# Casts of paired projections three slots apart, maxima's scores behind the first scores, values' bank copied by ScalarE, and single-bank PSUM tiles in the first and last phase of an attention and MLP kernel

## The chip, the cores and the metric

One core of a Trainium2 chip. The metric is the device time of one execution in microseconds (us); several executions are measured and the median is quoted. The core has five engines with a queue of instructions each: TensorE (PE in the profile; PEld is its loading of weights, which overlaps matmuls), VectorE (DVE), ScalarE (ACT), GpSimd (POOL) and SyncE (SP, which here only issues DMAs). Matmul results go to PSUM, which this kernel treats as eight banks of [128, 512] fp32; everything else lies in SBUF. A kernel written in the Tile language states which tile an instruction reads and writes, and the scheduler sets the semaphores: an instruction that writes a tile waits for the readers of what was there before.

## The reference, cut to what matters

S = 2048 tokens, D = 512, 32 heads of 16, window 256, MLP width 1792, all in fp32:

```python
xn = layernorm(x)
q, k, v = heads(xn @ wqkv)                       # H = 32, Dh = 16
scores = q @ k.T * 16 ** -0.5
scores = where(0 <= i - j < 256, scores, -1e9)   # i: query, j: key
s = heads_back(softmax(scores) @ v) @ wo
h = gelu(layernorm(xn) @ w1 + b1)                # tanh form of GELU
g = silu(h @ w2 + b2)
out = x + s * g
```

Both branches start from `xn`; the MLP branch normalises it once more.

## The kernel before, in words

**Precision.** Every product of activations and weights is made of three passes (`PASSES`, line 66): an operand is split by `split` (68) into a high part in `fp32r` and the low rest, and high x high, high x low and low x high are summed in PSUM. So each projection is 4 x 3 = 12 matmuls for a block of 128 x 512.

**Order.** All instructions are issued through `Ordered` (32 to 46), which holds TensorE, VectorE, ScalarE and GpSimd to the order of the program; only SP's queue is ordered by the scheduler. Since that helper records every operation, all rows of the profile carry its line, L42, and are told apart by the tiles' names. The order of the work is written out by hand in slots: a main loop over steps t = -16 to 128 (616 to 635), with two lists of work for each step. `fills[t, half]` holds matmuls that fill TensorE between the attention's own (projections, and later the first blocks of the MLP), `plan[t]` holds the rest (`at`, 523). A step of the loop issues, in this order: the scores and exponential of the second pair of heads (`prob_block(…, 1)`), the first half of the fill, the row maxima of the step 12 ahead (`max_block`, m = t + 12), the second half of the fill, the plan's entries, `prob_block(…, 0)`, and the values of the step before (`pv_step`).

**First phase (head, t < 0).** Layer norm of `x` by chunks of 512 tokens, transposes (`job_x`, 183), projections of the first group of four heads (`job_qk`, 239) and of the values (`job_v`, 277). There are eight groups of four heads (`NQ`); queries and keys of a group lie in a slot `qk0` or `qk1`, used in turn.

**Attention steps (t = 0 to 127).** 16 steps for each group, one for each block of 128 tokens. A step makes the scores of 128 keys against up to 384 queries transposed, into `stb` (`prob_block`, 425), the exponential by ScalarE into `pt`, and POOL masks `pt` by `affine_select`. The maximum of each row goes into the product as further rows of `qk`; `max_block` (384) makes it ahead: eight score matmuls, those of the farthest key block (`first`) into `zo`, the others into `xy`; then VectorE's `copy_predicated` merges the two under the triangular mask and `tensor_reduce` makes the maximum. After every fourth block `max_rows` (409) sends the rows to `qk` by way of DRAM. `pv_step` (446) multiplies the values with `pt` into `otb`, a part of `zo`'s second bank, VectorE copies `otb` to `oraw`, and every fourth step a DMA takes it to `oT_d`. The last 12 steps have no maxima left, and there every second scores go to `xy`.

**The paired projections.** From the second group on, two chunks are projected in tandem (`tandem`, 351): 64 contracted rows at a time, one chunk in the upper half of TensorE's rows and the other in the lower, into `fb[0]` and `fb[1]`. Each ends in `finish` (305): ScalarE copies the bank to `raw` (a tile of the pool `t2`, five buffers). Then `high` casts it to `fp32r` into `sh` and issues four DMAs of 128 KB into `qk` (from the third group on one of 16 KB more), and `low` lets POOL subtract into `sl` and issues two DMAs. `sh` and `sl` have one buffer each. When `high` and `low` run is set by lines 323 and 324, `at(t + 1 + c % 2, …)`: the plan of the first step after the pair's end for the even chunk, of the second for the odd one. There are 14 pairs of chunks (seven groups, two pairs each; spans in 576 to 579).

**PSUM before.** One pool holds eight banks for the whole run (153 to 157): `xy`, `zo` and `stb` are tiles of two banks, `fb[0]` and `fb[1]` of one. `bank()` (160) gives the two halves of `stb` in turn, or `fb[0]` and `fb[1]`. In the head `stb` serves transposes (kt 0 and 1) and values, then the attention's scores; the transposes of kt 2 and 3 go to `zo[:, 1]` and to `xy[:, 0]` or `fb`.

**Last phase (from 641).** The MLP by four chunks of 512 tokens, 14 blocks of hidden units each. `hidden` (688) makes a block in a half of `stb`, `activate` (693) applies GELU on ScalarE and splits on VectorE, `project` (702) adds its product with `w2` onto four accumulators, `accs = [xy[:, 0], xy[:, 1], zo[:, 0], fb[0]]` (684). At the end of a chunk (748 to 773) VectorE adds `b2` onto the accumulators, ScalarE applies SiLU (`gate`, two buffers in turn), TensorE transposes the next chunk's `y` into `zo[:, 1]` and `fb[1]` (`y_transpose`, 502), and four output products of 12 matmuls each go to halves of `stb`; each is multiplied by its gate on VectorE, added to `x` on POOL and sent out. Here "a boundary" is the stretch from the last `project` of a chunk to the first `project` of the next.

Of the kernel before, what the change touches and what calls it, by code (L numbers as in the profile page):

```python
# [9 lines left out]
F32 = mybir.dt.float32  # L10
# [8 lines left out]
P = 128  # L19
# [4 lines left out]
NQ = H // 4  # L24
# [25 lines left out]
def mixer_kernel(ctx, tc, x, wqk, wv, wo, w1, b1, w2, b2, out):  # L50
# [6 lines left out]
    t2 = ctx.enter_context(tc.tile_pool(name="t2", bufs=5))  # L57
    small = ctx.enter_context(tc.tile_pool(name="small", bufs=3))
    dram = ctx.enter_context(tc.tile_pool(name="dram", bufs=1, space=bass.MemoryType.DRAM))
    psum = ctx.enter_context(tc.tile_pool(name="psum", bufs=1, space=PSUM))  # L60
    attn = ExitStack()
    vp = attn.enter_context(tc.tile_pool(name="vp", bufs=1))
    pp = attn.enter_context(tc.tile_pool(name="pp", bufs=8))
    sgp = attn.enter_context(tc.tile_pool(name="sgp", bufs=1))
# [88 lines left out]
    xy = psum.tile([P, 2, 512], F32, name="xy")  # L153
    zo = psum.tile([P, 2, 512], F32, name="zo")
    otb = zo[:, 1, 256:384]
    stb = psum.tile([P, 2, 512], F32, name="stb")
    fb = [psum.tile([P, 512], F32, name=f"fb{i}") for i in range(2)]
    turn = {"st": 0, "fb": 0}

    def bank(kind="st"):  # L160

        turn[kind] ^= 1
        return stb[:, turn[kind]] if kind == "st" else fb[turn[kind]]

    vt = vp.tile([P, NKB, 16, DH + 1], F32, name="vt")

# [8 lines left out]
    mhalf = const.tile([P, 4], F32, name="mhalf")  # L175
    negc = const.tile([P, 1], F32, name="negc")
    nc.vector.memset(negc, NEG)
    mask = upper.bitcast(I32).unsqueeze(1).unsqueeze(1).to_broadcast([P, 2, 2, P])
    neg = negc.unsqueeze(2).unsqueeze(2).to_broadcast([P, 2, 2, P])
    b1s = const.tile([P, NF], F32, name="b1s")  # L180
# [2 lines left out]
    def job_x(c):  # L183
        box = []

        def mm(k):
            kt, i = k // 4, k % 4
            if i == 0:
                box.append(bank() if kt < 2 else zo[:, 1] if kt == 2 else xy[:, 0] if c == 0 else bank("fb"))
            nc.tensor.transpose(box[kt][:, P * i: P * (i + 1)], xs[c][i][:, P * kt: P * (kt + 1)], ident)  # L190
            if i == 3:
                sl = slice(512 * c, 512 * (c + 1))
                split(big[:, 0, kt, sl], big[:, 1, kt, sl], box[kt])
        return [(109, mm, k) for k in range(16)], lambda: None
# [44 lines left out]
    def job_qk(n, c):  # L239

        box = []
        ops = [(kt, a, b) for kt in range(KT) for a, b in PASSES]
        sl = slice(512 * c, 512 * (c + 1))

        def mm(i):
            if i == 0:
                box.append(bank("fb"))
            kt, a, b = ops[i]
            nc.tensor.matmul(box[0], wqs[n][:, a, kt], big[:, b, kt, sl],
                             start=(i == 0), stop=(i == len(ops) - 1))  # L250

        def send(src, qk, tt):
            copy_rows(slots[n % 2][tt:P:4, qk, :, sl], src[64 * qk: 64 * qk + 64])

        def finish():
            hi = sgp.tile([P, 512], F32R, tag="sh", name=f"sh_{n}_{c}")
            lo = sgp.tile([P, 512], F32R, tag="sl", name=f"sl_{n}_{c}")
            raw = t2.tile([P, 512], F32, tag="t2", name=f"pjr_{n}_{c}")
            nc.scalar.copy(raw, box[0])

            def high():
                nc.scalar.copy(hi, raw)
                if n >= 2:
                    copy_rows(slots[n % 2][3:P:32, 0, :, sl], slots[n % 2][7:P:32, 0, :, sl])
                for qk, tt in ((1, 0), (0, 0), (1, 2), (0, 1)):
                    send(hi, qk, tt)

            def low():
                (nc.gpsimd if n else nc.vector).tensor_tensor(lo, raw, hi.bitcast(F32), op=ALU.subtract)
                send(lo, 1, 1)  # L270
                send(lo, 0, 2)

            later(1 if n else 0, high)
            later(3 if n else 1, low)
        return [(216, mm, i) for i in range(len(ops))], finish

    def job_v(hf, i):

        box = []

        def mm(k):
            if k == 0:
                box.append(bank().rearrange("p (b d) -> p b d", b=2))
            j, kt, (a, b) = k // 12, k % 12 // 3, PASSES[k % 3]
            kb = 2 * i + j
            nc.tensor.matmul(box[0][:, j], big[:, a, kt, P * kb: P * (kb + 1)], wva[:, b, kt],
                             start=(k % 12 == 0), stop=(k % 12 == 11))

        def finish():
            nc.scalar.copy(vt[:, 2 * i: 2 * i + 2, :, 0:DH], box[0].rearrange("p b (h d) -> p b h d", d=DH))  # L290
        return [(109, mm, k) for k in range(24)], finish

    def pair_qk(n, c):

        ops = [(kt, a, b) for kt in range(KT) for a, b in PASSES]
        sl = slice(512 * c, 512 * (c + 1))

        def mm(ps, i, r, **flags):
            kt, a, b = ops[i]
            nc.tensor.matmul(ps, wqs[n][r, a, kt], big[r, b, kt, sl], **flags)  # L300

        def send(src, qk, tt):
            copy_rows(slots[n % 2][tt:P:4, qk, :, sl], src[64 * qk: 64 * qk + 64])

        def finish(ps, t):
            hi = sgp.tile([P, 512], F32R, tag="sh", name=f"sh_{n}_{c}")
            lo = sgp.tile([P, 512], F32R, tag="sl", name=f"sl_{n}_{c}")
            raw = t2.tile([P, 512], F32, tag="t2", name=f"pjr_{n}_{c}")
            nc.scalar.copy(raw, ps)

            def high():
                nc.scalar.copy(hi, raw)
                if n >= 2:
                    copy_rows(slots[n % 2][3:P:32, 0, :, sl], slots[n % 2][7:P:32, 0, :, sl])
                for qk, tt in ((1, 0), (0, 0), (1, 2), (0, 1)):
                    send(hi, qk, tt)

            def low():
                nc.gpsimd.tensor_tensor(lo, raw, hi.bitcast(F32), op=ALU.subtract)
                send(lo, 1, 1)  # L320
                send(lo, 0, 2)

            at(t + 1 + c % 2, high)
            at(t + 1 + c % 2, low)
        return 3 * KT, mm, finish

    def pair_v(i):
# [56 lines left out]
    def max_block(n, qb):  # L384
# [10 lines left out]
                         (xy[:, a, 256 * p + off: 256 * (p + 1)], slice(P * lo, P * (qb + 1))))  # L395
            nc.tensor.matmul(out, slot[r, 0, p, P * qb: P * (qb + 1)], slot[r, 1, p, keys], start=True, stop=True)

        for p, a, first in ((0, 1, True), (0, 0, False), (1, 1, True), (1, 0, False),
                            (0, 1, False), (1, 1, False), (0, 0, True), (1, 0, True)):
            if qb >= 2 or not first:  # L400
                scores(p, a, first)
        four = xy.rearrange("q a (p k) -> q a p k", p=2)
# [22 lines left out]
    def prob_block(n, kb, p):  # L425
        slot = slots[n % 2]
        w = min(384, S - P * kb)
        pt = pp.tile([P, 2, 384], F32, tag="pt", name=f"pt_{n}_{kb}_{p}")
        both = xy if p and 16 * n + kb + LEAD >= 16 * NQ else stb
        for a in (1, 0):  # L430
            r = slice(64 * a, 64 * a + 64)
            nc.tensor.matmul(both[:, a, 0:w], slot[r, 1, p, P * kb: P * (kb + 1)],
# [13 lines left out]
    def pv_step(n, qb):  # L446
# [7 lines left out]
                                 skip_group_check=True, tile_position=(0, 32 * j))  # L454
        if qb % 4 == 0:
            outs[0] = sgp.tile([P, 512], F32, tag="or", name=f"oraw_{n}_{qb}", bufs=2)
        nc.vector.tensor_copy(outs[0][:, P * (qb % 4): P * (qb % 4 + 1)], otb)
        if qb % 4 == 3:
            nc.sync.dma_start(oT_d[n // 2, n % 2::2, :, P * (qb - 3): P * (qb + 1)], outs[0])

# [41 lines left out]
    def y_transpose(c, kt, ps=None):  # L502
        ts = mlp["y"]
        if ps is None:
            ps = zo[:, 1] if kt % 2 else fb[1]
        for i in range(4):
            nc.tensor.transpose(ps[:, P * i: P * (i + 1)], ts[i][:, P * kt: P * (kt + 1)], ident)
        split(mlp["yy"][0][kt], mlp["yy"][1][kt], ps)
# [108 lines left out]
    for t in range(-16, end + 1):  # L617
        m = t + LEAD
        if t == -5:
            open_slot(1)  # L620
            clear_rows(1)
        if 0 <= t < end:
            prob_block(t // 16, t % 16, 1)
        fill_in(t, 0)
        if 0 <= m < end:
            max_block(m // 16, m % 16)
        fill_in(t, 1)
        for fn, args in plan.get(t, []):
            fn(*args)
# [11 lines left out]
    open_w2(1)  # L641
    gated = bigp.tile([P, 2, 512], F32, tag="wa", name="gated")
    attn.close()
    cp = ctx.enter_context(tc.tile_pool(name="cp", bufs=1))
    gp = ctx.enter_context(tc.tile_pool(name="gp", bufs=2))
    mlp["yp"] = ctx.enter_context(tc.tile_pool(name="yp", bufs=4))
    b2s = cp.tile([P, 512], F32, name="b2s")
    nc.sync.dma_start(b1s, b1)
    early = {}
    for f in range(0, EARLY, 2):  # L650
        t = gp.tile([P, 2, 512], F32, tag="ohl", name=f"hr_{f}", bufs=4)
        nc.sync.dma_start(t, h_d[f: f + 2].rearrange("f p t -> p f t"))
        early.update({f + 2: t[:, 0], f + 3: t[:, 1]})
    nc.sync.dma_start(b2s, bass.AP(tensor=b2.tensor, offset=b2.offset, ap=[[0, P], [1, 512]]))
    wos = cp.tile([P, 2, 4, 512], F32R, name="wos")
    for f in range(W2_FIRST, W2_FIRST + 2):
# [24 lines left out]
        return ohl  # L681

    for c in range(NCH):
        accs = [xy[:, 0], xy[:, 1], zo[:, 0], fb[0]]
        gs, os_, hs = {}, [], {}
        made = early if c == 0 else {}

        def hidden(f):
            hs[f] = bank()
            for k in range(3 * KT):  # L690
                hidden_mm(hs[f], f, k)

# [9 lines left out]
        def project(f):  # L702
            gh, gl = gs.pop(f)
            for i in range(4):
                acc = accs[i]
                sl = slice(P * i, P * (i + 1))
                for k, (a, b) in enumerate(((gh, 0), (gh, 1), (gl, 0))):
                    nc.tensor.matmul(acc, a[:, sl], w2_part(b, f), start=(f == 0 and k == 0),
# [4 lines left out]
        for f in range(NF + 1):  # L713
# [31 lines left out]
                os_.append(split_o(c, f - 11, *wanted))  # L745
            if 10 <= f < 14:
                wanted = load_o(c, f - 10)
        us = [accs[i] for i in range(4)]
        for u in us:
            nc.vector.tensor_add(u, u, b2s)  # L750

# [5 lines left out]
        for i in range(4):  # L757
# [2 lines left out]
                    y_transpose(c + 1, 2 * i + kt)  # L760
            tok = 512 * c + P * i
            xt = load(t2, "t2", x[tok: tok + P, :], f"xo_{c}_{i}")
            ps = bank()
            k = 0
            for g in range(4):
                for a, b in PASSES:
# [40 lines left out]
```

## Time and profile before

| | |
|---|---|
| three runs | 961.39, 955.6, 956.57 us; median 956.57 us |
| the profiled execution's own time | 956.07 us |
| its span on the core, mean granted TensorE clock | 954.3 us, 0.939 of full speed |
| busy over the span: PE, PEld | 800.4 us (84%), 615.7 us |
| DVE, ACT, POOL | 491.7 us (52%), 349.8 us (37%), 289.1 us (30%) |
| DMA | 29% of 16 engines' span, 84 GB/s |

By stage (times from the span's start): the head is 0 to 85.81 us, the attention steps 85.81 to 538.40, the first MLP chunk with the loading of the last weights 538.40 to 651.70, and the rest, three chunks and the four ends, 651.70 to 954.30.

How rows are read. A row of the busy time by stage has the stretch, its length, then busy us and instructions of PE, PEld, DVE, ACT and POOL, then the mean granted clock, the share of DMA and GB/s. A row of the waits has the waiting group, what it waited for, the us lost in sum, how often, and the mean of one. A row in order of time has the start, the duration, the engine, the instruction with its tiles (out<-in) and shape, how many are grouped, and in brackets how long the engine stood idle before it and for whom. A row of the groups has the busy time and the mean of one in ns, then the idle time before them and for whom.

### The profile page before, as it was taken

How to read it: one execution, taken by the hardware profiler on the slowest of the kernel's cores; microseconds unless marked ns; L12 is line 12 of the kernel's file. 1: busy time of each engine (PE TensorE's matmuls, PEld its weight loads, DVE VectorE, ACT ScalarE, POOL GpSimd, SP SyncE). 2: the span in 40 equal slices, each digit the busy share in tenths (PEclk: the TensorE clock that was granted, in tenths of full speed). 3: DMA queues.
4: the chain of work that ended last, by engine and by line, in shares of the span. 5: the costliest groups of instructions: out<-in, count | busy, mean ns of one | idle time of the engine just before them, and what ended most of it. 6: DMA issues, size and time to landing. Idle time of an engine off the chain costs nothing. (4 is left out here: it accounts for less than half of the span.)

```text
span 954.3 us, 18265 instructions
## 1 busy us (share of the span) xinstructions
PE 800.4 (84%) x7384; PEld 615.7 (65%) x7384; DVE 491.7 (52%) x866; ACT 349.8 (37%) x515; POOL 289.1 (30%) x575
## 2 busy tenths in 40 slices
PE   4789887778889888887788889579996899779995
PEld 4677555555667667555565578457885688658883
DVE  6666656667656556666676275421543144521242
ACT  5523545545555454544557622211111111111110
POOL 4001544545454344554565400120012101120012
PEclk9889989989999999888799999889999999899999
DMA  8332343332452223335415352420013001210022
GB/s 289 86 64 64 82 103 105 91 86 67 105 126 50 72 54 112 92 82 133 116 37 156 115 176 89 132 78 12 23 46 125 28 5 40 89 44 1 23 76 79
DMA packets 51476, 79.97 MB, mean 84 GB/s; under 512 B 10112, under 2 KB 14208, under 8 KB 51392
## 3 DMA queue, kind: packets, MB, share of 16 engines
q1 hardware_dynamic: 51392, 78.80, 29.0%
q8 instruction: 58, 0.95, 0.5%
q14 instruction: 26, 0.21, 0.1%
HBM read 35.13 MB, written 15.99 MB: 54 GB/s over the span
## 5 line engine op out<-in xcount | busy, mean ns | idle before, releaser
L42 POOL TENSOR_SCALAR_AFFINE_SELECT pt<-pt 128x256 f32<-128x256 f32 x480 | 188.5, 418 | 223.1 <-ACT pt L42 222.2
L42 ACT ACTIVATE pt<-stb 128x768 f32<-128x768 f32 (+1 forms) x244 | 189.0, 775 | 163.4 <-PE stb L42 153.8
L42 DVE TENSOR_REDUCE mt<-xy 128x4 f32<-128x1024 f32 (+1 forms) x128 | 152.6, 1192 | 4.4
L42 DVE COPY_PREDICATED xy<-upper,zo 128x512 f32<-128x512 int32 x112 | 78.0, 696 | 141.5 <-PE zo L42 136.8
L42 PE MATMUL stb<-yh,w1s 128*128 128x512 f32 x400 | 132.6, 394 | 7.6 <-ACT g L42 5.0
L42 PE MATMUL stb<-qk 64*128 64x384 f32 (+1 forms) x488 | 101.7, 409 | 42.0 <-ACT pt L42 38.9
L42 PE MATMUL zo<-pt,vt 128*17 128x128 f32 x2880 | 109.2, 285 | 23.8 <-DVE xy L42 21.2
L42 PE MATMUL fb<-xnT,wqb 64*128 64x512 f32 (+1 forms) x720 | 129.1, 425 | 0.0
L42 DVE CAST gh<-g 128x512 fp32r<-128x512 f32 x56 | 26.9, 480 | 165.1 <-ACT g L42 155.6
L42 PEld LDWEIGHTS zo<-pt,vt 128*17 128x17 f32 x2880 | 70.0, 100 | 64.1 <-DVE xy L42 51.6
L42 ACT ACTIVATE g<-stb,b1s 128x512 f32<-128x512 f32 x50 | 34.0, 689 | 205.1 <-PE stb L42 201.8
L42 PEld LDWEIGHTS stb<-qk 64*128 64x128 f32 x488 | 49.3, 196 | 80.0 <-ACT pt L42 69.5
L42 PE MATMUL xy<-qk 64*128 64x256 f32 (+2 forms) x536 | 90.6, 320 | 3.9 <-DMA qk<-sl 3.5
L42 PEld LDWEIGHTS stb<-yh,w1s 128*128 128x128 f32 x400 | 75.9, 190 | 26.2 <-ACT g L42 6.3
L42 PEld LDWEIGHTS zo<-qk 64*128 64x128 f32 x448 | 70.5, 203 | 25.6 <-DVE oraw L42 19.0
L42 PEld LDWEIGHTS xy<-qk 64*128 64x128 f32 x536 | 75.3, 204 | 8.7 <-issue 5.3
L42 PE MATMUL zo<-qk 64*128 64x128 f32 x448 | 74.7, 270 | 6.1 <-DVE oraw L42 5.6
L42 PE MATMUL stb<-w1s 128*128 128x512 f32 x200 | 78.6, 393 | 0.0
L42 PE MATMUL xy<-w,gh 128*128 128x512 f32 x224 | 70.3, 394 | 9.1 <-DVE gh L42 4.4
L42 PEld LDWEIGHTS fb<-xnT,wqb 64*128 64x128 f32 (+1 forms) x720 | 73.2, 202 | 4.9
L42 POOL TENSOR_TENSOR or<-or,rec 128x512 f32<-128x512 f32 x16 | 20.5, 1284 | 150.2 <-DMA rec<-rden_d 134.4
L42 PE MATMUL stb<-wos,ohl 128*128 128x512 f32 x192 | 56.7, 450 | 9.8 <-DVE gated L42 9.0
(108 smaller groups left out, 1045.2 us busy)
## 6 DMA issues: line engine op xcount, KB each, us to landing
qk<-sh SPq DMA_DIRECT2D x128, 128.0 KB
qk<-sl SPq DMA_DIRECT2D x64, 128.0 KB
oT_d<-oraw SPq DMA_DIRECT2D x32, 256.0 KB
x<-in_x_dram SPq DMA_DIRECT2D x16, 256.0 KB
or<-oT_d SPq DMA_DIRECT2D x16, 256.0 KB
rec<-rden_d SPq DMA_DIRECT2D x16, 256.0 KB
xo<-in_x_dram SPq DMA_DIRECT2D x16, 256.0 KB
out_dram<-xo SPq DMA_DIRECT2D x16, 256.0 KB
```

Of the source, the lines that this page charges most:

```text
L42: r = issue(*args, **kwargs)
```

## The change

Four things, in the one file:

- **Casts.** `high` and `low` of the odd chunk of a pair run in the plan of the fourth step after the pair's end instead of the second.
- **Maxima.** `max_block` is called right behind `prob_block(…, 1)`, ahead of the fill's first half. Its eight matmuls are reordered: the four into `xy` first, the four into `zo` last.
- **Copy.** `oraw<-otb` is made by ScalarE; `otb` is cleared once at the start.
- **PSUM.** The pool of the attention now ends with it. In the head two tiles of one bank (`ps_st`) serve the transposes kt 0 and 1 and the values; the transposes kt 2 and 3 go to `fb` in turn with the projections. At t = 0 these two tiles give way to the two-bank `stb`. In the last phase three pools of two tiles each take the eight banks: `ps_mx` (two banks a tile, the four accumulators), `ps_st` (one bank: hidden blocks and output products) and `ps_yt` (one bank: the transposes of `y`). The dictionary `early` is renamed `ready`.

```diff
-    psum = ctx.enter_context(tc.tile_pool(name="psum", bufs=1, space=PSUM))
     attn = ExitStack()
+    psum = attn.enter_context(tc.tile_pool(name="psum", bufs=1, space=PSUM))
...
-    stb = psum.tile([P, 2, 512], F32, name="stb")
     fb = [psum.tile([P, 512], F32, name=f"fb{i}") for i in range(2)]
-    turn = {"st": 0, "fb": 0}
-
-    def bank(kind="st"):
-
-        turn[kind] ^= 1
-        return stb[:, turn[kind]] if kind == "st" else fb[turn[kind]]
+    early = ExitStack()
+    ps_st = early.enter_context(tc.tile_pool(name="ps_st", bufs=2, space=PSUM))
+    stb = []
+    turn = [0]
+
+    def fill_bank():
+
+        turn[0] ^= 1
+        return fb[turn[0]]
...
+    nc.vector.memset(otb, 0.0)
...
-                box.append(bank() if kt < 2 else zo[:, 1] if kt == 2 else xy[:, 0] if c == 0 else bank("fb"))
+                box.append(ps_st.tile([P, 512], F32, tag="b", name=f"tr_{c}_{kt}") if kt < 2 else fill_bank())
...
-                box.append(bank("fb"))
+                box.append(fill_bank())
...
-                box.append(bank().rearrange("p (b d) -> p b d", b=2))
+                box.append(ps_st.tile([P, 2, 256], F32, tag="b", name=f"pv_{hf}_{i}"))
...
-            at(t + 1 + c % 2, high)
-            at(t + 1 + c % 2, low)
+            at(t + 1 + 3 * (c % 2), high)
+            at(t + 1 + 3 * (c % 2), low)
...
-        for p, a, first in ((0, 1, True), (0, 0, False), (1, 1, True), (1, 0, False),
-                            (0, 1, False), (1, 1, False), (0, 0, True), (1, 0, True)):
+        for p, a, first in ((0, 1, False), (0, 0, False), (1, 1, False), (1, 0, False),
+                            (0, 1, True), (0, 0, True), (1, 1, True), (1, 0, True)):
...
-        both = xy if p and 16 * n + kb + LEAD >= 16 * NQ else stb
+        both = xy if p and 16 * n + kb + LEAD >= 16 * NQ else stb[0]
...
-        nc.vector.tensor_copy(outs[0][:, P * (qb % 4): P * (qb % 4 + 1)], otb)
+        nc.scalar.copy(outs[0][:, P * (qb % 4): P * (qb % 4 + 1)], otb)
...
-            ps = zo[:, 1] if kt % 2 else fb[1]
+            ps = ps_yt.tile([P, 512], F32, tag="b", name=f"yt_{c}_{kt}")
...
         if 0 <= t < end:
+            if t == 0:
+                early.close()
+                stb.append(attn.enter_context(tc.tile_pool(name="ps_s2", bufs=1, space=PSUM)).tile(
+                    [P, 2, 512], F32, name="stb"))
             prob_block(t // 16, t % 16, 1)
-        fill_in(t, 0)
         if 0 <= m < end:
             max_block(m // 16, m % 16)
+        fill_in(t, 0)
         fill_in(t, 1)
...
     attn.close()
+    ps_mx = ctx.enter_context(tc.tile_pool(name="ps_mx", bufs=2, space=PSUM))
+    ps_st = ctx.enter_context(tc.tile_pool(name="ps_st", bufs=2, space=PSUM))
+    ps_yt = ctx.enter_context(tc.tile_pool(name="ps_yt", bufs=2, space=PSUM))
...
-        accs = [xy[:, 0], xy[:, 1], zo[:, 0], fb[0]]
+        accs = [ps_mx.tile([P, 2, 512], F32, tag="mx", name=f"acc_{c}_{i}") for i in range(2)]
...
-            hs[f] = bank()
+            hs[f] = ps_st.tile([P, 512], F32, tag="b", name=f"h_{c}_{f}")
...
-                acc = accs[i]
+                acc = accs[i // 2][:, i % 2]
...
-            ps = bank()
+            ps = ps_st.tile([P, 512], F32, tag="b", name=f"s_{c}_{i}")
```

More of the change, by code (lines that the diff above doesn't have):

```diff
@@ L648, in mixer_kernel @@
     nc.sync.dma_start(b1s, b1)
-    early = {}
+    ready = {}
     for f in range(0, EARLY, 2):
@@ L652, in mixer_kernel @@
         nc.sync.dma_start(t, h_d[f: f + 2].rearrange("f p t -> p f t"))
-        early.update({f + 2: t[:, 0], f + 3: t[:, 1]})
+        ready.update({f + 2: t[:, 0], f + 3: t[:, 1]})
     nc.sync.dma_start(b2s, bass.AP(tensor=b2.tensor, offset=b2.offset, ap=[[0, P], [1, 512]]))
@@ L683, in mixer_kernel @@
     for c in range(NCH):
-        accs = [xy[:, 0], xy[:, 1], zo[:, 0], fb[0]]
+        accs = [ps_mx.tile([P, 2, 512], F32, tag="mx", name=f"acc_{c}_{i}") for i in range(2)]
         gs, os_, hs = {}, [], {}
-        made = early if c == 0 else {}
+        made = ready if c == 0 else {}
         def hidden(f):
-            hs[f] = bank()
+            hs[f] = ps_st.tile([P, 512], F32, tag="b", name=f"h_{c}_{f}")
             for k in range(3 * KT):
@@ L747, in mixer_kernel @@
                 wanted = load_o(c, f - 10)
-        us = [accs[i] for i in range(4)]
+        us = [accs[i // 2][:, i % 2] for i in range(4)]
         for u in us:
```

## Prediction

> **What bounds the kernel now.** I read the page first, then the busy time by stage (windows), then who waited for whom in each stage, and last the order in time around the longest waits.
>
> ```profile
> core 0: us, PE busy (x) PEld busy (x) DVE busy (x) ACT busy (x) POOL busy (x), PEclk, DMA share, GB/s
> 0.00:85.81 85.81, 64.36 (x412) 53.95 (x414) 52.20 (x100) 33.37 (x53) 10.91 (x22) 0.92 0.48 136
> 85.81:538.40 452.59, 377.00 (x5438) 274.00 (x5434) 282.61 (x484) 244.20 (x354) 230.59 (x514) 0.92 0.35 92
> 651.70:719.78 68.08, 68.08 (x302) 56.30 (x301) 28.65 (x58) 10.14 (x14) 5.88 (x5) 1.00 0.11 34
> 719.78:756.80 37.02, 25.31 (x107) 19.38 (x106) 10.66 (x17) 7.07 (x11) 6.40 (x5) 0.95 0.23 80
> 823.50:861.94 38.44, 25.89 (x101) 19.63 (x100) 10.28 (x16) 6.38 (x10) 6.40 (x5) 0.87 0.14 53
> ```
>
> TensorE is the busiest engine. The stages differ. Inside an MLP chunk (651.70 to 719.78) it is never idle and the clock granted is 1.00, so nothing is to be had there. Between two chunks (the last two rows) it is busy about 25 of 37 to 38 us. In the attention steps (85.81 to 538.40, 128 steps) and in the head it loses 75 and 21 us, at a mean clock of 0.92. The change touches these three.
>
> Who waits in the attention steps, and one such wait in order of time:
>
> ```profile
> ACT sh L42 <- DMA qk<-sh: 38.2, 14, 3.7
> PE stb L42 <- ACT pt L42: 38.9, 27, 3.4
> PE zo L42 <- DVE xy L42: 21.2, 58, 0.7
> ```
> ```profile
> 304.67 0.61 ACT L42 CAST sh<-pjr 128x512 fp32r<-128x512 f32 x1
> 311.16 0.62 ACT L42 CAST sh<-pjr 128x512 fp32r<-128x512 f32 x1 [3.00 <-DMA qk<-sh]
> 312.54 0.38 PE L42 MATMUL stb<-qk 64*128 64x256 f32 x2 [2.45 <-ACT pt L42]
> ```
>
> The reader should see a queue. The second cast of a pair comes one step after the first into the same buffer `sh`, whose four transfers are not done; ScalarE stands 3.00 us, the exponential behind the cast is late, and the next scores, which need the bank that it reads, leave TensorE idle for 2.45. There are 14 such casts, one per pair of projections. What one costs in whole steps (start of one exponential to that of another, two steps each):
>
> ```profile
> 116.20:122.24 6.04, 5.49 (x88) 3.89 (x84) 4.76 (x10) 4.62 (x8) 3.77 (x9) 1.00 0.11 14
> 122.24:133.82 11.58, 7.99 (x90) 5.74 (x88) 4.67 (x9) 3.77 (x6) 4.95 (x11) 0.73 0.61 157
> 445.52:452.54 7.02, 4.17 (x52) 2.28 (x48) 5.29 (x9) 4.62 (x7) 4.43 (x10) 0.94 0.52 149
> 452.54:462.56 10.02, 6.79 (x72) 4.64 (x72) 4.93 (x11) 3.76 (x5) 4.29 (x9) 0.50 0.62 161
> ```
>
> The first such place costs 11.58 - 6.04 = 5.5, the last 10.02 - 7.02 = 3.0; part is the wait, part the clock, which falls after it (0.73, 0.50). Over 13 of the 14 places, each against the two steps ahead of it, it comes to 46 us. The 14th, step 4, is held by something else (below).
>
> **The casts three slots apart.** The high cast and the subtraction of the odd job move from two steps after the pair's end to four; the even job's stay at one. With them go six transfers of 128 KB and, from the third group on, one of 16 KB. On SP's queue they go behind a transfer of row maxima and one of `oT_d`; on POOL the subtraction goes behind the masks of two more steps; the raw tile is held two steps longer in a pool of five, of which at most three are live then. From 304.67 to 311.16 the buffer was busy 6.5 us; three steps of 3.0 us (6.04 / 2) are 9, so the wait ends before the cast comes. Once (steps 50 and 52) only two steps lie between: up to 1 us left. If all goes, 46 us; if only TensorE's idle time goes, 38.2 x 2.45 / 3.00 = 31. I take 46, since half of a place's price is the clock that falls with it.
>
> What comes late instead is the data. A chunk's odd half is first read six to thirteen steps after the old cast, except in the first group (old cast in step 4, new in step 6, read in step 8). Step 4 shows how long that takes:
>
> ```profile
> 96.48 0.61 ACT L42 CAST sh<-pjr 128x512 fp32r<-128x512 f32 x1
> 102.84 0.44 PE L42 MATMUL xy<-qk 64*128 64x128 f32 x4 [3.49 <-DMA qk<-sl]
> ```
>
> 6.4 us from cast to use; from the plan's place in step 6 to the start of step 8 are some 5 us (one step and two thirds), so about 1.5 us at step 8. In step 4 the maxima's scores now stand ahead of the fill, which no longer covers: 0.5. Together 2 us lost (0 to 5).
>
> **Maxima behind the first scores; the bank copied by ScalarE.** The order of instructions on TensorE changes from scores, fill, maxima's scores, fill, scores, values to scores, maxima's scores, fill, fill, scores, values; the maxima's eight matmuls write `xy` first and `zo` last. VectorE's masked copy then has both fills as cover before the values need `zo`. In the row above TensorE lost 21.2 us to that copy, but most of that is not on the path: the next scores wait for the second exponential anyway.
>
> ```profile
> 302.35 0.83 ACT L42 ACTIVATE pt<-stb 128x768 f32<-128x768 f32 x1
> 302.62 0.85 PE L42 MATMUL zo<-pt,vt 128*17 128x128 f32 x24 [0.63 <-DVE xy L42]
> 303.39 0.44 PE L42 MATMUL stb<-qk 64*128 64x384 f32 x2
> ```
>
> Here the values waited 0.63, but the exponential ended at 303.18, so the scores at 303.39 came only 0.2 later than it allowed: a third. Between 0 and 21 I take 8.
>
> The copy of `otb` (128x128) leaves VectorE and joins ScalarE between two exponentials. No row has it on ScalarE:
>
> ```profile
> L42 DVE COPY oraw<-zo 128x128 f32<-128x128 f32 x128 | 36.1, 282 | 12.3 <-PE zo L42 12.1
> L42 ACT ACTIVATE pt<-stb 128x256 f32<-128x256 f32 x15 | 5.9, 392 | 8.1 <-PE stb L42 7.5 <-POOL pt L42 0.5
> ```
>
> ScalarE takes 0.39 for 256 elements and 0.83 for 768 (the row at 302.35), 0.11 for each 128, so 128 are about 0.28 (an estimate from these two rows), at most 0.39. The cover is the time in which TensorE makes the next scores, 0.44 us (the row at 303.39). Without that cover it costs its whole length; that is the case in the last 12 steps, which have no maxima and where ScalarE goes from one piece to the next:
>
> ```profile
> 517.16 0.82 ACT L42 ACTIVATE pt<-stb 128x768 f32<-128x768 f32 x1
> 517.87 0.81 ACT L42 ACTIVATE pt<-xy 128x768 f32<-128x768 f32 x1
> 518.56 0.63 ACT L42 CAST w1s<-w1r 128x512 fp32r<-128x512 f32 x1
> ```
>
> 12 x 0.25 = 3 us lost (0 to 4.7). The copy holds up who is queued behind it: the next exponential, hence the masks on POOL. The new clear of `otb` lies in VectorE's idle start: nothing.
>
> **Single-bank tiles, first phase.** In the head, transposes, values and scores share the two-bank tile `stb`, and a writer of one bank waits for the readers of the other.
>
> ```profile
> PE stb L42 <- DVE xnT L42: 8.0, 5, 2.7
> PE zo L42 <- DVE xy L42: 2.7, 2, 1.4
> PE stb L42 <- ACT vt L42: 2.0, 3, 0.7
> ```
>
> With a tile to each bank these 12.7 us go, but two transposes now share `fb` with the projections and wait for their copies, and the first maxima move ahead of a projection. Between 3 and 13 I take 8.
>
> **Single-bank tiles, last phase.** How often TensorE waited so, and the third boundary in order of time:
>
> ```profile
> PE zo L42 <- DVE zo L42: 17.6, 3, 7.2
> ```
> ```profile
> 823.50 0.60 PE L42 MATMUL fb<-ident,y 128*128 128x128 f32 x4
> 827.06 0.69 DVE L42 TENSOR_TENSOR ohl<-or,ohl 128x512 fp32r<-128x512 f32 x1
> 829.75 1.12 PE L42 MATMUL zo<-ident,y 128*128 128x128 f32 x4 [5.65 <-DVE zo L42]
> 830.51 4.64 PE L42 MATMUL stb<-wos,ohl 128*128 128x512 f32 x12
> 830.72 0.69 DVE L42 TENSOR_TENSOR w1s<-fb,yh 128x512 fp32r<-128x512 f32 x1 [0.43 <-ACT yh L42]
> 838.37 3.00 PE L42 MATMUL stb<-wos,ohl 128*128 128x512 f32 x12
> 842.15 3.03 PE L42 MATMUL stb<-wos,ohl 128*128 128x512 f32 x12 [0.78 <-DVE gated L42]
> 857.73 0.62 PE L42 MATMUL stb<-yh,w1s 128*128 128x512 f32 x1 [2.12 <-ACT g L42]
> ```
>
> The transposes into `zo`'s second bank wait 5.65 us for an addition in its first; each output product waits for the gate of the one before it, though the banks alternate; the third hidden matmul waits for the activation of the first. With tiles of their own the first two transposes run at 823.5; the first product follows and ends at 828.4, 0.7 after the last `ohl` (827.06 + 0.69). The third transpose waits for its bank until VectorE's subtraction ends, 830.72 + 0.69 = 831.4, and the fourth for the next one, 0.7 later: this pause of 3 us is next. The second product starts at 832.6, takes 4.4 if the clock falls (4.64 at 830.51, against 3.00 at 838.37), and ends at 837.0. Two more products and three hidden blocks follow, 12 matmuls each, 12 x 68.08 / 302 = 2.7 us: 850.5. Before, the third hidden block ended at 861.94. The gates hold nothing: VectorE multiplies at 832.1, 837.0 and 839.7, each before its bank is due. That is 11 us at this boundary. The first row has the wait at each of the three boundaries, so I take 33 for all.
>
> At the very end:
>
> ```profile
> 937.03 4.33 PE L42 MATMUL stb<-wos,ohl 128*128 128x512 f32 x12 [2.63 <-DVE gated L42]
> 949.20 0.69 DVE L42 TENSOR_TENSOR gated<-stb,gated 128x512 f32<-128x512 f32 x1 [3.17 <-PE stb L42]
> ```
>
> Without the wait the second product starts at 937.03 - 2.63 = 934.4, the last multiplication comes three products later, at 942.5 instead of 949.20: 7. Together 40 us (25 if another wait takes each pause's place).
>
> **The sum** is made against the profiled execution: its own time is 956.07, its span 954.3, and the median of the runs is 956.57. 956 - 8 (head) - 46 (casts) - 8 (maxima) + 3 (ScalarE) + 2 (late data) - 40 (chunks) = 859 us.
>
> **Rivals.**
> - The pause of 3 us does not lower the clock. For it: the second boundary has the same waits and a granted clock of 0.95 (0.87 at the third). Then three products take 3.0 instead of 4.4: 859 - 4 = 855. Against it: the pause of 2.63 us at 937.03 is followed by a product of 4.33. [...]
> - The steps stay long: the transfers of the pair run into each other at three slots too, or ScalarE's copy lengthens each step, and of the 49 us net in the steps only 15 come: 893. For it: DMA share 0.61 in such steps. Against it: the 6.5 us of buffer time.
> - The last phase is held by the gate's chain over ScalarE and POOL, so that tiles of their own change less: 25 instead of 40, 874. Against it: the times of the chain above.
> - Slower: ScalarE's copy waits for the values' matmuls, which wait for POOL's masks, and all exponentials queue behind it. POOL is busy 230.59 of 452.59 us. It decides from 97 / 116 = 0.84 us of delay in each step with maxima; at 1 us the time is 859 + 116 = 975. Against it: the values rarely wait for POOL, and its masks have a step's time.
>
> **How the numbers follow.** The forecast has 0.56, the clock rival 0.15, long steps 0.14, the gate's chain 0.09, slower or nothing gained 0.06. The time is 859. Its own bounds are 841 (13 in the head, 21 by the maxima) to 879 (31 by the casts, 3 in the head); the range reaches a little beyond them to the rivals at 855, 874 and 893: 838 to 895. Faster by over 1% (which is about what a measurement here can tell from no change) 0.94, within it 0.02, slower 0.04.
>
> **What would show it.** Right: ScalarE's wait for `qk<-sh` near zero; the attention steps near 404 us instead of 452.59 and their clock above 0.95; boundaries of 26 to 29 us with no wait of a product for the gate one before it; the head near 78. Wrong: long waits for `qk<-sl` or `qk<-sh` at the scores, exponentials that wait for ScalarE's copy, or a clock that stays at 0.92.

## The result, and the profile after

The changed kernel takes 841.46 us (median of 4 runs, 841.03 to 842.4) against 956.09 us before (4 runs measured beside it): a ratio of 0.8792, 95% interval 0.8759 to 0.8824. The forecast was 859, with a range of 838 to 895: the way and the size were right, and the gain of 115 us is 18 more than forecast. The profiled execution took 841.03 us, its span 839.3 us. Here and below a time is the median of all executions, while a ratio leaves out the few that fell in a slower state of the chip (two of ten for the maxima alone, one of the 19 measured beside them).

Busy time by stage of the changed kernel: the head, the attention steps (from the first exponential of step 0 to that of step 127), the three boundaries between chunks, and the end after the last projection; then the same stages of the kernel before where the prediction did not show them.

```profile
0.00:72.35 72.35, 59.26 (x413) 49.93 (x415) 51.63 (x102) 32.83 (x53) 10.91 (x22) 1.00 0.57 162
72.35:470.78 398.43, 353.12 (x5410) 259.51 (x5410) 261.90 (x355) 271.35 (x477) 228.75 (x513) 0.99 0.41 104
545.88:577.20 31.32, 23.66 (x102) 19.01 (x99) 12.33 (x20) 6.88 (x11) 7.02 (x6) 0.84 0.35 109
645.36:666.10 20.74, 20.74 (x102) 17.31 (x99) 9.55 (x16) 6.88 (x11) 5.16 (x4) 1.00 0.34 123
734.26:755.08 20.82, 20.82 (x101) 17.27 (x99) 9.64 (x16) 6.88 (x11) 5.16 (x4) 1.00 0.19 75
823.24:839.30 16.06, 10.89 (x49) 8.67 (x47) 5.29 (x8) 2.29 (x4) 5.13 (x4) 0.97 0.26 96
```
```profile
85.81:537.07 451.26, 375.77 (x5411) 273.25 (x5409) 282.58 (x483) 242.91 (x352) 230.18 (x513) 0.92 0.35 92
612.25:651.77 39.52, 26.77 (x101) 20.24 (x99) 11.40 (x18) 6.38 (x10) 7.66 (x6) 0.83 0.26 87
719.95:755.50 35.55, 23.84 (x101) 18.11 (x100) 10.28 (x16) 6.38 (x10) 6.40 (x5) 0.95 0.24 82
823.66:862.17 38.51, 25.96 (x101) 19.66 (x99) 10.28 (x16) 6.38 (x10) 6.40 (x5) 0.87 0.14 52
930.34:954.30 23.96, 13.62 (x49) 9.35 (x47) 6.29 (x10) 2.28 (x4) 6.41 (x5) 0.91 0.22 81
```

The span is 954.3 - 839.3 = 115.0 us shorter: 13.5 in the head, 52.8 in the steps, 40.7 at the boundaries (113.6 to 72.9), 7.9 at the end; the stages between differ by 0.1. At the last two boundaries TensorE is now busy all the time. The granted clock went up with it (0.92 to 0.99 in the steps), and the same 7384 matmuls that kept TensorE busy for 800.4 us at a mean clock of 0.939 take 760.6 at 0.983: about 40 of the 115 us are busy time, and the rest is idle time.

All of TensorE's waits in the attention steps of the changed kernel:

```profile
PE stb L42 <- ACT pt L42: 26.6, 46, 1.4
PE xy L42 <- DMA qk<-sl: 6.7, 3, 4.2
PE zo L42 <- DVE xy L42: 1.7, 5, 0.5
PE stb L42 <- DMA w1r<-in_w_dram: 0.7, 1, 0.7
PE xy L42 <- DVE mt L42: 0.5, 2, 0.3
PE fb L42 <- ACT hr L42: 0.2, 1, 0.2
```

ScalarE's 38.2 us of waits for the transfers of `sh` are gone from its list, and of the 21.2 us in which the values waited for the masked copy 1.7 are left. The waits for the transfers of `sl`, the data that come late, grew from 3.5 us in one wait to 6.7 in three.

### The profile page after: what moved, and what is told of

Its sections match the earlier page's. It is cut to its first block, busy times and chain, and to the rows that moved or that the text cites. A ratio compares the mean times of both kernels' runs of the same rounds, so it can differ in the third digit from the quotient of the medians.

```text
span 839.3 us, 18438 instructions
## 1 busy us (share of the span) xinstructions
PE 760.6 (91%) x7384; PEld 594.0 (71%) x7384; DVE 467.6 (56%) x739; ACT 378.3 (45%) x643; POOL 288.3 (34%) x575
## 5 line engine op out<-in xcount | busy, mean ns | idle before, releaser
L42 PE MATMUL acc<-w,gh 128*128 128x512 f32 x448 | 141.5, 396 | 6.3 <-DVE gh L42 3.7
L42 PE MATMUL h<-yh,w1s 128*128 128x512 f32 x400 | 130.3, 389 | 0.4 <-ACT oraw L42 0.4
L42 PE MATMUL stb<-qk 64*128 64x384 f32 (+1 forms) x488 | 95.7, 386 | 35.9 <-ACT pt L42 26.6
L42 ACT ACTIVATE g<-h,b1s 128x512 f32<-128x512 f32 x50 | 34.5, 690 | 185.9 <-PE h L42 182.5
L42 PEld LDWEIGHTS acc<-w,gh 128*128 128x128 f32 x448 | 85.5, 191 | 26.6 <-DVE w L42 3.4
L42 PE MATMUL acc<-w,gl 128*128 128x512 f32 x224 | 88.5, 395 | 0.0
L42 PEld LDWEIGHTS h<-yh,w1s 128*128 128x128 f32 x400 | 75.1, 188 | 16.2 <-ACT oraw L42 0.7
L42 PE MATMUL h<-w1s 128*128 128x512 f32 x200 | 77.8, 389 | 0.0
L42 PE MATMUL xy<-qk 64*128 64x256 f32 (+2 forms) x536 | 61.9, 304 | 10.1 <-DMA qk<-sl 6.7
L42 PEld LDWEIGHTS xy<-qk 64*128 64x128 f32 x536 | 45.3, 186 | 21.2 <-issue 9.1
L42 PE MATMUL s<-wos,ohl 128*128 128x512 f32 x192 | 47.3, 403 | 4.9 <-DVE ohl L42 4.9
```

The lines of the kernel that those rows point to most:

```text
L42: r = issue(*args, **kwargs)
```

## The experiments

First single parts of the change on the kernel before, then the changed kernel with one part undone, then two attempts at what was left.

**Casts alone.**

```diff
-            at(t + 1 + c % 2, high)
-            at(t + 1 + c % 2, low)
+            at(t + 1 + 3 * (c % 2), high)
+            at(t + 1 + 3 * (c % 2), low)
```

> The kernel before with one edit: the odd chunk's cast and subtraction three slots after the even one's. If the terms of the forecast stand by themselves (46 us for the casts, 2 us lost to late data), 912 us. Rival: with the old order of the maxima VectorE's chain of copy and maximum is the next to end a step, and only TensorE's idle time of 31 us goes: 925 to 930 us. In both ScalarE's 38.2 us of waits for the transfers of sh are near zero.

913.9 us, ratio 0.9574 (0.9506 to 0.9641). The attention steps, in the row of this run, and what ScalarE waited for in them:

```profile
86.23:492.83 406.60, 358.07 (x5411) 257.36 (x5408) 284.37 (x483) 242.37 (x351) 229.61 (x513) 0.98 0.40 102
```
```profile
ACT pt L42 <- PE stb L42: 143.6, 179, 4.4
ACT pt L42 <- POOL sl L42: 7.1, 10, 0.9
ACT pt L42 <- POOL pt L42: 6.8, 11, 0.9
```

451.26 - 406.60 = 44.7 us go in the steps; no wait for `sh` is left, and the clock rises from 0.92 to 0.98. Measured as in the prediction, each of the 13 places against the two steps ahead of it, the places' excess falls from 46.2 to 0.4 us. So the whole price of a place goes, not TensorE's idle time alone.

**Only the subtraction late.** The second of the two changed lines alone.

> The kernel before with half of that edit: only the subtraction of the odd chunk (POOL, into sl) moves by two steps, the cast (ScalarE, into sh) stays where it was. The forecast blames the cast's wait on ScalarE (38.2 us in 14 waits): then nearly nothing is gained, 950 to 957 us. Rival: the subtraction's wait on POOL for the transfers of sl (32.2 us in 9 waits, with masks queued behind it) is what lengthened the steps: 920 to 930 us.

956.09 us against 955.66, ratio 1.0003 (0.9975 to 1.0032): nothing. ScalarE's wait stands as before, while POOL's wait of 32.2 us for the transfers of `sl` is not among the waits any more:

```profile
ACT sh L42 <- DMA qk<-sh: 36.4, 14, 3.7
```

So the cast's wait on ScalarE is enough by itself to lengthen the steps; POOL's almost equally long wait for the same pairs lay beside it and added nothing. What POOL's wait would cost without the cast's was not tried: the subtraction reads what the cast writes, and so can't stay while the cast moves.

**The maxima's place and order alone.**

```diff
-        fill_in(t, 0)
         if 0 <= m < end:
             max_block(m // 16, m % 16)
+        fill_in(t, 0)
         fill_in(t, 1)
```

and the new list of the eight matmuls.

> The kernel before with two edits of the maxima alone: called right behind the first scores, and the four matmuls into xy ahead of the four into zo. Forecast: 8 us, 948 us. Rivals: 956 us if the second exponential sets the step anyway; 936 us if all of the 21.2 us goes in which TensorE waited with the values for VectorE's masked copy.

951.1 us, ratio 0.9934 (0.9894 to 0.9973): some 6 us, between 3 and 10. In the profiled execution the head is 2.4 us shorter (first exponential at 83.39) and the steps 5.2 (446.03; in the runs with the subtraction alone, the last phase alone and the head alone, which leave this order as it was, the steps took 449.6, 448.1 and 449.1, so that part of the 5.2 is scatter). The two waits of TensorE that the prediction listed for the steps show what happens:

```profile
PE stb L42 <- ACT pt L42: 57.0, 47, 3.5
PE zo L42 <- DVE xy L42: 2.1, 5, 0.6
```

The wait for the masked copy falls from 21.2 to 2.1 us, as meant, but the wait for the exponential rises from 38.9 to 57.0: most of the time only changes its name.

**The last phase's tiles alone.** `ps_mx`, `ps_st` and `ps_yt` as in the change, with the head's PSUM as before.

> The kernel before with the last phase's pools of single banks alone (accumulators of two banks, one bank each for hidden blocks, output products and transposes of y). The changed kernel's last phase, from the first projection of the MLP to the end, is 48.6 us shorter; if the pools do it all, 907 us. The forecast's term was 40: 916 us. Rival: part of the 48.6 us comes from loads of rec that landed earlier for another reason: 915 to 925 us.

901.47 us, ratio 0.9444 (0.9385 to 0.9503). The same four stretches:

```profile
607.87:639.91 32.04, 24.58 (x101) 19.67 (x99) 12.33 (x20) 6.88 (x11) 6.87 (x6) 0.84 0.32 107
708.08:729.44 21.36, 21.08 (x101) 17.23 (x99) 10.22 (x17) 6.88 (x11) 5.14 (x4) 1.00 0.34 123
797.60:819.26 21.66, 21.07 (x101) 17.23 (x99) 10.48 (x17) 6.88 (x11) 5.15 (x4) 1.00 0.19 73
887.42:903.50 16.08, 10.89 (x49) 8.68 (x47) 5.05 (x8) 2.28 (x4) 5.13 (x4) 0.96 0.25 95
```

38.5 us at the boundaries and 7.9 at the end, 46.4 of the 48.6: the tiles do it, the rival's "other reason" is left with 2 us. (The profile's span is 50.8 us shorter; 3.1 of the rest lie in the attention steps, which this edit leaves alone, and are scatter.)

**The head's tiles alone.** `ps_st` in the head, `fb` for kt 2 and 3, `stb` from t = 0, and the clear of `otb`.

> The kernel before with the head's part alone: two tiles of one bank for the transposes kt 0 and 1 and the values, kt 2 and 3 in fb, the two-bank stb only from t = 0. The changed kernel's head is 13.5 us shorter (85.81 to 72.35 us). If these tiles do it all: 943 us. Forecast: 8 us, 948. Rival: a part of the 13.5 us comes from the maxima's new place in the head's steps, and the tiles give 3 to 6: 950 to 953 us. The start of the first exponential says it without the rest.

940.46 us, ratio 0.9835 (0.9756 to 0.9914). The head of this run:

```profile
0.00:71.45 71.45, 60.08 (x414) 50.18 (x416) 51.26 (x101) 32.82 (x53) 10.91 (x22) 1.00 0.57 163
```

14.4 us shorter: the tiles alone give it all, and the maxima's place, worth 2.4 there alone, adds nothing to them. Of the 14.4 us, 10.1 are idle time: of the 12.7 us of waits that the prediction counted the like of 2.3 are left (0.8 for the first maxima, 0.8 for `xnT`, 0.7 for `vt`). The other 4.3 are the clock: it was 0.92 and is 1.00, and the busy time falls from 64.36 to 60.08 us.

**The changed kernel with the maxima's old place and order.** The reverse of the third edit.

> The changed kernel with the maxima's old place and old order of matmuls. If the terms add up, it loses what they gained alone, about 5 us: 846 us. Rival: with the casts' waits gone VectorE's chain ends the steps, so that the new order is worth more now: 852 to 860 us.

841.08 us, ratio 0.8801 (0.8742 to 0.8859): no difference from the changed kernel. The steps take 400.19 instead of 398.43 us, within the scatter seen above. The same two waits in them:

```profile
PE zo L42 <- DVE xy L42: 25.2, 69, 0.8
PE stb L42 <- ACT pt L42: 9.8, 25, 0.9
```

In the changed kernel they are 1.7 and 26.6 us. Again the order decides which of the two TensorE waits for, and hardly how long: its idle time in the steps is 46.7 us here and 45.3 in the changed kernel.

**The changed kernel with the copy on VectorE.**

```diff
-        nc.scalar.copy(outs[0][
+        nc.vector.tensor_copy(outs[0][
```

> The changed kernel with the copy of otb back on VectorE. Forecast: ScalarE's copy costs 3 us in the last 12 steps and nothing before, so 838 us. Rival: VectorE's copy stood between its maxima (36.1 us in 128 copies, and 20.2 us in which the load of values' weights waited for it), so that its going is a gain: 850 to 860 us.

843.74 us, ratio 0.883 (0.8773 to 0.8888), which overlaps that of the changed kernel. Its steps, and then its last 12 alone (with the same stretch of the changed kernel worked out from the starts of the exponentials: 23.34):

```profile
73.08:476.33 403.25, 357.00 (x5411) 262.31 (x5410) 289.65 (x481) 243.35 (x352) 228.35 (x513) 0.98 0.41 103
453.19:476.33 23.14, 22.64 (x373) 15.20 (x370) 8.94 (x22) 20.35 (x32) 16.18 (x44) 1.00 0.38 111
```

Undoing the copy makes the steps 4.8 us longer (one profile each; 399.06 in the run with `wo` loaded earlier, below, which keeps the copy) and the last 12 shorter by 0.2. So the copy on ScalarE is not the loss that was forecast: with that loss this run would have come to 838 us, below all of its executions (842.19 to 844.46). That it is a small gain is what the trace suggests; the times alone don't show it.

**The changed kernel with two slots instead of three.** `2 * (c % 2)` in both lines.

> The changed kernel with the odd chunk's cast and subtraction two slots after the even one's, not three. The buffer was busy 6.5 us from cast to cast, and two steps of 2.8 to 3.0 us are 5.6 to 6.0: ScalarE waits 0.5 to 0.9 us at each of 14 places, hidden in part: 843 to 852 us. Rival: the transfers take 4 us or less once the steps run on, two slots are enough, and the data come a step earlier: 836 to 841 us.

841.1 us, ratio 0.8805 (0.8745 to 0.8866): the same. ScalarE waits for the transfers of `sh` twice, 2.0 us in all; steps 4, 8 and 12 take 8.45, 3.36 and 4.45 us against 8.88, 5.04 and 4.11. What two slots win on late data they give back elsewhere. Two slots are nearly enough. The buffer's 6.5 us were those of one place: in the kernel before it was busy 4.97 to 7.40 us from cast to cast, and here all casts but two wait for no transfer.

**The changed kernel with the casts' old places.**

> The changed kernel with the casts' old places, one and two steps after the pair's end. Alone the new places gave 42 us (the casts-only run). If the parts add up: 841 + 42 = 883 us, with ScalarE's waits for the transfers of sh back near 38 us. Rival: the faster steps and the maxima's new place take part of the same waits: 865 to 878 us. If the steps are shorter, the buffer is still busy for the same 6.5 us and the wait is longer: 885 to 895 us.

885.13 us, ratio 0.9235 (0.9181 to 0.9288). Against the changed kernel's 0.8792 that is 0.0443 of 956, 42 us, as much as the same edit gave on the kernel before. The wait is back:

```profile
ACT sh L42 <- DMA qk<-sh: 35.9, 14, 3.4
```

**Attempt: wo loaded earlier.** The first boundary is 10 us longer than the others. There ScalarE's cast of the last `wo` tile waits 8.68 us for its load, and the loads of `or` and `rec` come late. The edit takes the four tiles out of the pool `t2`; `gated`, which uses the same buffer, is allocated behind the first chunk's last split.

```diff
+    def open_wo():
+        mlp["wo"] = bigp.tile([P, 4, 512], F32, tag="wa", name="wor")
+        for g in range(4):
+            nc.sync.dma_start(mlp["wo"][:, g], wo[:, 512 * g: 512 * (g + 1)])
...
+    at(114, open_wo)
...
-        raw = load(t2, "t2", wo[:, 512 * g: 512 * (g + 1)], f"wor{g}")
-        split(wos[:, 0, g], wos[:, 1, g], raw)
+        split(wos[:, 0, g], wos[:, 1, g], mlp["wo"][:, g])
```

> The changed kernel with the four tiles of wo loaded during the attention's last steps into a buffer of their own (the one that the gates use later), not into t2 in the first chunk. In the changed kernel the first boundary is 31.31 us and the others 20.74 and 20.82; there the cast of the last wo tile on ScalarE waits 8.68 us for its load, the activation queues behind it, and the last loads of rec land 6 us after the chunk's end. If that is the cause, the first boundary comes near 21 us: 831 us. Rival: the loads of or and rec are late for want of t2 buffers anyway: 838 to 841 us.

838.95 us, ratio 0.8771 (0.8734 to 0.8808), which overlaps 0.8792. The first boundary is 30.9 us as before, so the theory of it fell: the last `or` waits for the load of `rec` without the `wo` tiles too.

```profile
547.18 1.26 POOL L42 TENSOR_TENSOR or<-or,rec 128x512 f32<-128x512 f32 x1 [4.95 <-DMA rec<-rden_d]
```

The chunks outside the boundaries, from the first projection of the MLP on, take 264.0 us in this profile, 262.5 in the other one with this edit (both attempts together) and 268.8 in that of the changed kernel. Among the runs with the new tiles that leave `wo` alone they vary from 265.0 to 270.2, so a gain of a few us there is possible, but the times don't show it. That the loads lack `t2` buffers anyway was not tried by itself.

**Attempt: casts earlier.** `at(t + 2 * (c % 2), …)`: in the step of the pair's end and two later.

> The changed kernel with each cast earlier: the even chunk's in the plan of the step in which the pair ends, the odd one's two steps later (before: one and four steps after it). If late data cost what the long steps 4, 8 and 12 show (8.88, 5.04 and 4.11 us against about 2.9), up to 9 us go: 832 to 836 us. Rival: two slots are too few for the transfers, or the cast stands between the copies of the banks and the second exponential: 841 to 850 us.

846.21 us, ratio 0.8844 (0.8808 to 0.8879): some 5 us slower than the changed kernel, with intervals that just overlap, and so hardly shown, though step 4 falls from 8.88 to 3.19 and step 12 from 4.11 to 3.05. Waits come in place of it, in small pieces over the steps:

```profile
POOL sl L42 <- ACT sh L42: 20.5, 18, 2.3
ACT sh L42 <- DMA qk<-sh: 5.6, 5, 2.2
PE stb L42 <- DMA qk<-qk: 2.8, 3, 1.1
```

There the cast stands between the copies of the banks and the second exponential (in the first such step the copies start at 80.84, the cast at 81.80, the exponential at 82.31). And both attempts together:

> The changed kernel with both edits, the early load of wo and the earlier casts. If both stand and don't touch each other, the sum of their gains: 822 to 827 us. Rival: only one of them holds: 831 to 836 us.

843.99 us, ratio 0.8822 (0.8789 to 0.8854): no better than the changed kernel. None of the versions beats it beyond the intervals.

## Why the prediction was right, and where it was not

| Term | forecast | measured |
|---|---|---|
| head | -8 | -13.5; the tiles alone -14.4 |
| casts, net of late data | -46 + 2 | -44.7 in the steps (casts alone), -42 (undone) |
| maxima's place and order | -8 | alone some -6 (-7.6 in the trace), nothing beside the other parts |
| copy on ScalarE | +3 | no loss; -4.8 in the steps of one profile |
| boundaries | -33 | -40.7 |
| end | -7 | -7.9 |

The terms miss in both directions: head, boundaries and copy came out better than forecast, by 5.5, 7.7 and up to 7.8 us, the maxima up to 8 worse. That the sum is only 18 off is in part luck. Of the signs that the prediction named, ScalarE's wait is gone and the steps take 399.55 us over the same stretch, against "near 404"; the head lies below its 78 (72.35), and no boundary lies in its 26 to 29 (31.32, 20.74, 20.82).

**The casts** were right in place, mechanism and size. The rival of long steps (893 us) is refuted: no cast into `sh` waits for a transfer any more, and the steps are 53 us shorter. That half of a place's price is the clock is roughly borne out: with the casts alone TensorE's busy time in the steps falls from 375.77 to 358.07 us, 18 of 44.7. The late data cost more than the 2 us: steps 4, 8 and 12 went from 7.26 + 3.11 + 3.34 to 8.88 + 5.04 + 4.11, 4.3 us longer. Some 1.5 of it, in step 4, come with the new order and not with the late cast: there the order alone makes 8.77 us and the casts alone 7.27. What the prediction said of step 8 came true with the number: a wait of 1.56 us against "about 1.5".

**The head** was too small by a term left out. Of 12.7 us of waits the prediction took 8, and 10.1 us of idle time went; the clock that falls after them, another 4.3 us, it did not count, although the casts' term had it.

**The copy** was priced as a loss and is none. Its length was right (0.27 us against 0.28; 12 of them are 3.4 and not 3), but in the last 12 steps it cost 0.2 us, and the prediction took nothing for the load it takes off VectorE: 36.1 us of copies between the maxima. The maxima's own matmuls into `zo` waited for them in the kernel before, and no longer; with the copy undone 3.4 us of waits for it in `zo` are back. That this is where the trace's 4.8 us come from is likely, not shown. The row of the kernel before:

```profile
L42 PE MATMUL zo<-qk 64*128 64x128 f32 x448 | 74.7, 270 | 6.1 <-DVE oraw L42 5.6
```

**The maxima**: the prediction gave the reason why most of the 21.2 us is no gain ("the next scores wait for the second exponential anyway"), and then took 8 of it between 0 and 21. The reason holds nearly whole: with the order alone 19.1 us of that wait go and 18.1 come back as waits for the exponential, and in the changed kernel undoing the order moves them the other way. Alone some 6 us are left, in the sum nothing that the times show; why the two differ was not tried.

**The boundaries** lost 8.2, 14.8 and 17.7 us where the prediction took 11 for each. The last two were mis-sized by one step of the working: "the first product follows and ends at 828.4, 0.7 after the last `ohl`", which left the old time of `ohl` as it was, and so a pause of 3 us behind it. The third boundary in the changed kernel:

```profile
732.75 0.43 DVE L42 CAST ohl<-or 128x512 fp32r<-128x512 f32 x1 [1.76 <-POOL or L42]
733.21 0.69 DVE L42 TENSOR_TENSOR ohl<-or,ohl 128x512 fp32r<-128x512 f32 x1
734.10 1.03 PE L42 MATMUL yt<-ident,y 128*128 128x128 f32 x8
734.89 2.98 PE L42 MATMUL s<-wos,ohl 128*128 128x512 f32 x12
736.87 1.29 DVE L42 TENSOR_TENSOR w1s<-yt,yh 128x512 fp32r<-128x512 f32 x2 [0.30 <-ACT yh L42]
737.72 1.16 PE L42 MATMUL yt<-ident,y 128*128 128x128 f32 x8
```

The last `ohl` is ready at 733.9, before the chunk's end at 734.26; in the kernel before it was ready at 827.75, 4.1 us behind the end at 823.66. So the first product covers the subtractions, the next transposes wait for nothing, and the clock stays at 1.00. Why `ohl` is early shows at the start of a chunk, ScalarE's activations before and after:

```profile
856.99 0.69 ACT L42 ACTIVATE g<-stb,b1s 128x512 f32<-128x512 f32 x1
862.37 0.69 ACT L42 ACTIVATE g<-stb,b1s 128x512 f32<-128x512 f32 x1 [4.70 <-PE stb L42]
867.87 0.69 ACT L42 ACTIVATE g<-stb,b1s 128x512 f32<-128x512 f32 x1 [4.81 <-PE stb L42]
```
```profile
751.18 0.69 ACT L42 ACTIVATE g<-h,b1s 128x512 f32<-128x512 f32 x1
752.57 0.69 ACT L42 ACTIVATE g<-h,b1s 128x512 f32<-128x512 f32 x1 [0.69 <-PE h L42]
755.33 0.69 ACT L42 ACTIVATE g<-h,b1s 128x512 f32<-128x512 f32 x1 [2.08 <-PE h L42]
```

With the shared `stb` the second activation waited until the third block of 12 matmuls was done (862.3), though its own block was done before 856; with tiles of their own it follows its block at once. Every activation of a chunk is one round (5.4 us) earlier. That its buffers in `t2`, which `or` and `rec` share, therefore come free earlier is the likely link to `ohl`; it was not tried by itself. The tiles alone show the same boundaries (21.36 and 21.66 us).

The first boundary (31.32 us) has a wait that the prediction did not have: the last load of `rec` lands 6 us after the chunk's end. Of the rivals, the gate's chain (874) is refuted: no product waits for a gate. ScalarE's copy as a brake (975) is refuted by the copy's own run. The clock rival (855) can't be judged at the last two boundaries, since the pause that it speaks of isn't there. The first boundary has it, 2.74 us in front of the third transposes, and the clock behind it is 0.50:

```profile
558.13 1.97 PE L42 MATMUL yt<-ident,y 128*128 128x128 f32 x8 [2.74 <-DVE w1s L42]
558.13:561.53 3.40, 3.40 (x12) 3.09 (x13) 1.14 (x2) 0.82 (x2) 1.27 (x1) 0.50 0.25 77
```

That settles nothing about the rival, for the clock was 0.50 already during this pause (557.50 to 558.00) and in the 1.65 us of work ahead of it (553.74 to 555.30), which follow the pause of 4.92 us for the last `ohl`.

## What to carry to other kernels

A tile that two users shared made each wait here for the other's whole round (5.4 us for each activation of a chunk): look not only for who waits at the tile, but for what runs one round late behind it. Price a stall by its wait and by the clock after it (10.1 and 4.3 us in the head), at every place and not only at the one under study. And where two long waits lie side by side (ScalarE's for `sh`, POOL's for `sl`), move one alone before blaming either.

## What the runs showed of the hardware

The granted clock was 0.50 also behind a pause shorter than the 3 us that the prediction reckoned with. In the changed kernel TensorE pauses for 1.86 us in front of 481.62; the clock by stretches:

```profile
479.70:481.62 1.92, 0.06 (x2) 0.00 (x1) 0.45 (x2) 0.69 (x1) 0.00 (x0) 1.00 0.16 60
481.62:483.40 1.78, 1.78 (x7) 1.18 (x8) 1.70 (x3) 0.00 (x0) 0.00 (x0) 1.00 0.69 179
483.40:486.80 3.40, 3.40 (x10) 2.63 (x9) 0.92 (x2) 1.34 (x2) 0.00 (x0) 0.50 1.01 370
486.80:490.20 3.40, 3.40 (x16) 2.81 (x15) 1.17 (x3) 1.23 (x2) 0.00 (x0) 1.00 0.91 279
```

The clock is 0.50 for 3.40 us, starting 1.8 us after work had begun again; 10 matmuls run in it against 16 in the next 3.40. The kernel before, though, has a pause of 2.37 us in front of 837.96, and the product behind it takes 3.00 us at a clock of 1.00 (838.37 to 841.40), against 4.64 at 830.51, where the granted clock is 0.50 until 834.1 (both rows are in the prediction). So the length of a pause alone doesn't decide; what else does was not shown.
